# A short arm for a second tile of at most 32 slots in a top-1 mixture of experts, and the last expert's further arms inside its first

## The chip, the cores and the metric

The kernel runs on one core of one Trainium2 chip. The metric is the device time of one execution in microseconds (us), given as the median of timed runs. Each core has five engines with instruction queues of their own: TensorE (PE; its weight loads are listed as PEld), VectorE (DVE), ScalarE (ACT), GpSimd (POOL) and SyncE (SP), which here only issues transfers. A name with a q behind it (PEq, POOLq) is the engine's sequencer, which also carries out branches and semaphore waits.

## The reference

Three stages run one after the other in one launch: attention (2 batches, 8 heads, 576 tokens, head size 64), a dense feed-forward layer (512 to 2048 to 512, ELU), and the mixture of experts, which the change is about. It has 1152 tokens, 8 experts, and a capacity of 288 tokens for each expert:

```python
logits = x @ w_gate                        # [1152, 8]
expert_idx = np.argmax(logits, axis=1)     # one expert for each token
gate_w = probs[np.arange(N), expert_idx]   # softmax of the logits
...                                        # disp[e, s] = the s-th token of expert e, up to capacity
h = np.maximum(np.einsum('ecd,edf->ecf', disp, w1), 0.0)   # 512 -> 1024
y = np.einsum('ecf,efd->ecd', h, w2)                       # 1024 -> 512
out[i] = gate_w[i] * y[expert_idx[i], pos[i]]              # zero for a token over capacity
```

How many tokens an expert gets is known only when the router has run.

## The kernel before, in words

Every product is made from float32 numbers split into a high and a low part, in three passes: high by high, high by low, low by high. A "split" is an ACT copy that makes the high part (`xh`, `gh`, `dh`) and a DVE subtraction that makes the low part (`xl`, `gl`, `dl`, all through the helper at L86).

The dense layer fills the stretch from about 96 to 317 us. There PE and SP follow an order written out by hand, while a scheduler chooses the order of DVE, ACT and POOL; the router's small constants are among what it places, `pair` (L732) with them, a [64, 32] sum of two pieces of the identity.

The experts fill the rest, in an order written out by hand on all engines. POOL writes each token's row (512 numbers, its gate and its index) to its slot in DRAM, `disp`. An expert's 288 slots are cut into tiles of 128, 128 and 32. For each expert `e`:

- SP loads the next expert's first tile of rows (`load_rows(e + 1, 0)`), and half of the weights of the expert after that (`load_x`). Raw weights wait in buffers `ra` and `rb` until they are split.
- `If(count[e] > 0)` (L1333) holds `compute(e, 0)`. PE multiplies 128 slots with the first weights in two halves of 512 columns (L1176, 12 matmuls each), turns the result (L1187), multiplies with the second weights (L1197, 24 matmuls), and between these the engines do side work: the split of the eight weight tiles of expert `e + 1`, `turn_slots(e, 1)` (PE turns the second tile of rows, L1146, ACT makes `dh`, DVE `dl`, POOL copies gate and index into `gt`, L1151 and L1152) and `turn_slots(e + 1, 0)`. The Else arm does the weight splits for an expert without tokens.
- Then SP loads `rows(e + 1, 1)`, into a buffer that POOL's copies of `gt` must have read, and the other half of the weights.
- `If(count[e] > 128)` (L1346) holds `compute(e, 1)`, the same on the second tile with no weights to split beside it. Inside it `If(count[e] > 256)` holds `compute_few(e, 2)` for the third tile: its 32 slots lie twice in one 64-wide operand, `ds`, high parts beside low parts, so that one pass takes the place of two (16, 8 and 16 matmuls: L1244, L1256 with `pair`, L1270).
- POOL sends each tile's result (L1294, an indirect DMA with one index for each slot; empty slots point out of bounds and write nothing).

Each If is a compare on PE, ACT, DVE and POOL apart. Where it is not taken, the engine jumps to a block that raises the semaphores that the skipped block would have raised; on POOL this includes an instruction `INC_SWDGE_SEM` for the skipped send.

## Time and profile before

| | us |
|---|---|
| median of 3 timed runs | 481.84 |
| lowest and highest | 480.65, 484.97 |
| the profiled execution's own time | 480.35 |
| its span, first to last instruction | 478.4 |
| PE busy | 459.9 (96%) |
| DVE busy | 352.1 (74%) |
| ACT busy | 300.1 (63%) |
| POOL busy | 97.9 (20%) |

The profile is of one execution. Its span leaves out some 2 us around the program, so a change of the span is read as the same change of the time. Spans on POOL are rough. Lines are those of the kernel before; the changed kernel's lines stand up to 35 further down.

### The profile page before, as it was taken

Reading aid. Unit: us, or ns where it says so; the run is one execution under the profiler, and the core shown is the slowest. Engines: PE = TensorE matmul, PEld = TensorE weight load, DVE = VectorE, ACT = ScalarE, POOL = GpSimd, SP = SyncE. Lnnn points to the kernel's source line nnn. Section 1 sums busy time; section 2 is a strip of 40 time slices with the busy share of each in tenths; the row PEclk is TensorE's granted clock in tenths of the full one; section 3 lists DMA queues with packets and bytes.
Section 4 is the critical chain, followed back from the end, with each engine's and each line's share of the span. In section 5 each row is a group of like instructions: output and inputs, shape, how many; then the busy total and the mean of one; then the engine's idle time right before and its main releaser. Section 6 shows DMA issues by size and latency. Waiting matters only on the chain. (4 is left out here: it accounts for less than half of the span.)

```text
span 478.4 us, 8177 instructions
## 1 busy us (share of the span) xinstructions
PE 459.9 (96%) x2708; PEld 384.1 (80%) x2708; DVE 352.1 (74%) x765; ACT 300.1 (63%) x660; POOL 97.9 (20%) x178
## 2 busy tenths in 40 slices
PE   7899999999999999999999999999999999999994
PEld 6777777789999999999998888878777877777773
DVE  7999999999989996974473465459388995561661
ACT  5999997967776665653553446447388883541640
POOL 3655666410000000000000020522120331210110
PEclk9999999999999999999999999999999999999999
DMA  7875786036898831330121032448979999260100
GB/s 210 225 205 153 215 249 189 6 135 185 254 299 273 285 135 44 135 130 1 35 99 46 1 110 76 173 130 310 403 241 360 354 357 333 93 228 22 29 27 26
DMA packets 34900, 81.10 MB, mean 170 GB/s; under 512 B 4642, under 2 KB 4642, under 8 KB 34848
## 3 DMA queue, kind: packets, MB, share of 16 engines
q1 hardware_dynamic: 33072, 75.44, 48.8%
q0 software_dynamic: 1632, 4.72, 2.6%
q8 instruction: 27, 0.44, 0.4%
q10 hardware_dynamic: 144, 0.29, 0.2%
q14 instruction: 25, 0.20, 0.2%
HBM read 64.49 MB, written 12.41 MB: 161 GB/s over the span
## 5 line engine op out<-in xcount | busy, mean ns | idle before, releaser
L259 PE MATMUL acc<-wbh,gh 128*128 128x512 f32 x144 | 57.2, 397 | 0.0
L259 PE MATMUL acc<-wbh,gl 128*128 128x512 f32 x144 | 56.8, 394 | 0.0
L259 PE MATMUL acc<-wbl,gh 128*128 128x512 f32 x144 | 56.7, 393 | 0.0
L884 POOL DMA_INDIRECT disp<-y_all,slot x9 | 9.1, 1016 | 198.6 <-DVE e L244 175.9
L242 ACT ACTIVATE e<-h 128x384 f32<-128x384 f32 x48 | 23.2, 484 | 40.1 <-PE h L232 37.7
L185 DVE SCALAR_TENSOR_TENSOR cv_t<-r,cv_t 128x512 int32<-128x512 int32 x64 | 45.4, 710 | 0.5
L452 ACT ACTIVATE prob<-s,stat 64x64 f32<-64x64 f32 (+3 forms) x80 | 41.3, 529 | 6.3 <-PE pT L494 3.0
L232 PE MATMUL h<-xh,wah 128*128 128x384 f32 x192 | 42.7, 342 | 0.6 <-DVE e L244 0.6
L86 DVE TENSOR_TENSOR xl<-ra,xh 128x1024 fp32r<-128x1024 f32 (+1 forms) x36 | 39.2, 1100 | 5.1 <-ACT xh L1096 3.9
L244 DVE SCALAR_TENSOR_TENSOR e<-e,h 128x384 f32<-128x384 f32 x48 | 26.3, 548 | 22.2 <-ACT e L243 21.9
L1096 ACT ACTIVATE xh<-ra 128x1024 fp32r<-128x1024 f32 (+1 forms) x36 | 34.2, 961 | 12.1 <-PEq L1346 8.5
L232 PE MATMUL h<-xh,wal 128*128 128x384 f32 x192 | 41.2, 337 | 0.0
L232 PE MATMUL h<-xl,wah 128*128 128x384 f32 x192 | 41.1, 336 | 0.0
L477 POOL TENSOR_SCALAR prob<-prob,stat 64x64 f32<-64x64 f32 (+2 forms) x64 | 32.6, 521 | 36.5 <-DVE stat L463 14.8
L232 PEld LDWEIGHTS h<-xh,wah 128*128 128x128 f32 x192 | 34.5, 188 | 5.7 <-issue 1.1
L86 DVE TENSOR_TENSOR xl<-rb,xh 128x1024 fp32r<-128x1024 f32 (+1 forms) x36 | 38.8, 1098 | 0.0
L1294 POOL DMA_INDIRECT out<-o,gt x12 | 17.6, 1465 | 100.8 <-DVE o L1229 48.9
L248 ACT ACTIVATE gh<-e 128x384 fp32r<-128x384 f32 x48 | 25.1, 524 | 20.0 <-DVE e L244 18.7
L1197 PE MATMUL acc<-xh,gh 128*128 128x512 f32 x88 | 36.3, 412 | 0.0
L444 DVE TENSOR_REDUCE stat<-s 128x1 f32<-128x320 f32 (+2 forms) x80 | 34.8, 476 | 0.8 <-PE s L426 0.5
L1197 PE MATMUL acc<-xl,gh 128*128 128x512 f32 x88 | 34.7, 395 | 0.0
L1197 PE MATMUL acc<-xh,gl 128*128 128x512 f32 x88 | 34.7, 395 | 0.0
(191 smaller groups left out, 1102.6 us busy)
## 6 DMA issues: line engine op xcount, KB each, us to landing
ra<-in_moe_w SPq DMA_DIRECT2D x32, 512.0 KB, 5.3
rb<-in_moe_w SPq DMA_DIRECT2D x32, 512.0 KB, 5.9
r<-in_moe_w_in SPq DMA_DIRECT2D x16, 512.0 KB, 5.1
r<-in_moe_w_out SPq DMA_DIRECT2D x16, 512.0 KB, 4.4
disp<-z SPq DMA_DIRECT2D x18, 257.0 KB, 6.7
kr<-in_k SPq DMA_DIRECT2D x15, 288.0 KB, 4.0
rows<-disp SPq DMA_DIRECT2D x14, 257.0 KB, 3.4
v<-in_v SPq DMA_DIRECT2D x8, 320.0 KB, 4.5
```

The source lines that it names most:

```text
L86: eng.tensor_tensor(out=lo, in0=x, in1=hi.bitcast(FP32), op=ALU.subtract)
L185: nc.vector.scalar_tensor_tensor(out=st["t"], in0=x(), scalar=scalar, in1=st["t"], op0=op, op1=ALU.bitwise_or)
L232: nc.tensor.matmul(out=h[:, f, :], lhsT=w[:, kk, (f0 + f) * 128:(f0 + f + 1) * 128], rhs=x[:, kk, t0:t0 + n], start=(i == 0), stop=(i == l ...
L242: nc.scalar.activation(out=e, in_=hf, func=ACTF.Relu, scale=-1.0)
L244: nc.vector.scalar_tensor_tensor(out=e, in0=e, scalar=-1.0, in1=hf, op0=ALU.add, op1=ALU.max)
L248: nc.scalar.activation(out=gh, in_=ef, func=ACTF.Copy)
L259: nc.tensor.matmul(out=acc[t], lhsT=x[:, f, t * 128:(t + 1) * 128], rhs=w[:, f0 + f, :], start=(first and f == 0 and i == 0), stop=(last a ...
L444: nc.vector.tensor_reduce(out=stat[n][0][0:nq, t:t + 1], in_=x, axis=AX.X if part else AX.XY, op=ALU.max, negate=True)
L452: nc.scalar.activation(out=out if part else out.rearrange("p (b c) -> p b c", b=NB), in_=x, func=ACTF.Exp, bias=stat[n][0][0:nq, t:t + 1], ...
L477: eng.tensor_scalar(out=p, in0=p, scalar1=sc, scalar2=0.0, op0=ALU.mult, op1=ALU.add)
L1096: lambda: nc.scalar.activation(out=hi, in_=r, func=ACTF.Copy),
L1197: nc.tensor.matmul(out=acc[0:n], lhsT=x[:, f % 4, 0:n], rhs=y[:, f % 2, :], start=(f == 0 and i == 0), stop=(f == NF - 1 and i == 2),)
```

## The change

`FEW = 32` is new. A second tile of 128 slots gets a second operand `ds` (pool `few1`, [128, 4, 64]). `set_aside(1)` fills it with two POOL copies (called CAST in the rows of the order), the first 32 slots of the high and of the low part; it is called once at the start of the experts and then in each `turn_slots(e, 1)`, ahead of the two copies of `gt`. `further(e)` takes the place of the two nested Ifs: a second tile with over 32 tokens in it still gets `compute(e, 1)` and the third tile inside that; one with 1 to 32 gets `compute_few(e, 1)` in an Else. A second `pair` is made for it. For the last expert, `further` is called inside its first If.

```diff
+    FEW = 32
...
         for j, (_, n) in enumerate(FIRST):
-            if n > 64:
+            few = min(n, FEW)
+            if n > FEW:
                 state["dT"].append([pool_of["cnt"].tile([128, KD, n], F32R, name=f"d{x}{j}") for x in "hl"])
+            else:
+                both = state["dS"][j] = pool_of["cnt"].tile([128, KD, 2 * n], F32R, name=f"ds{j}")
+                state["dT"].append([both[:, :, 0:n], both[:, :, n:2 * n]])
+            if j == 0:
                 continue
...
+            n = few
             pair = state["pair"][j] = pool_of["cnt"].tile([2 * n, n], FP32, name=f"pair{j}")
...
+    def set_aside(j):
+
+        if j in state["dS"] and FIRST[j][1] > FEW:
+            for x, src in enumerate(state["dT"][j]):
+                nc.gpsimd.tensor_copy(
+                    out=state["dS"][j][:, :, x * FEW:(x + 1) * FEW], in_=src[:, :, 0:FEW].bitcast(FP32)
+                )
...
+        for j, (s0, n) in enumerate(stiles):
+            if j and n > FEW:
+                dS[j] = p3.enter_context(tc.tile_pool(name=f"few{j}", bufs=1, side="right")).tile(
+                    [128, KD, 2 * FEW], F32R, name=f"ds{j}"
+                )
+                set_aside(j)
...
             split_lo(nc.vector, lo, ps[:, :, 0:n], hi)
+            set_aside(j)
             nc.gpsimd.tensor_copy(out=gt[0:n, j, 0:1], in_=r[0:n, DM:DM + 1])
...
+        def further(e, j=1):
+
+            if j == CT:
+                return
+            s0, n = stiles[j]
+            with tc.If(count[e] > s0):
+                if n <= FEW:
+                    compute_few(e, j)
+                    return further(e, j + 1)
+                with tc.If(count[e] > s0 + FEW) as many:
+                    compute(e, j)
+                    further(e, j + 1)
+                with many.Else():
+                    compute_few(e, j)
...
             with tc.If(count[e] > 0) as some:
                 compute(e, 0, (his, los[:-LATE]), turn_next)
+                if not new:
+                    further(e)
...
-            with ExitStack() as arms:
-                for j in range(1, CT):
-                    arms.enter_context(tc.If(count[e] > 128 * j))
-                    (compute_few if j in dS else compute)(e, j)
+            if new:
+                further(e)
```

The program's order shows what this makes of three places. The first is PE between the fifth expert's first arm and the sixth expert's. Before, the second tile has one way to be computed; the rows are the start of that arm (`dh_1706` and `dl_1707` are the second tile's operands):

```order
L1346 COMPARE_AND_BRANCH
L1176 MATMUL hx<-xh,dh_1706 128x512 x4
L1176 MATMUL hx<-xl,dh_1706 128x512 x4
L1176 MATMUL hx<-xh,dl_1707 128x512 x4
L1146 MATMUL dT<-ident,rows 128x32 x4
L1176 MATMUL hx<-xh,dh_1706 128x512 x4
L1176 MATMUL hx<-xl,dh_1706 128x512 x2
```

Now that arm is followed by a second one in the program, on PE again, the start and end of which are (`ds_4045` is the new operand, `pair_1708` its pair):

```order
L1341 UNCONDITIONAL_BRANCH x2
L1264 MATMUL hx<-xh,ds_4045 64x512 x4
L1264 MATMUL hx<-xl,ds_4045 64x512 x4
L1264 MATMUL hx<-xh,ds_4045 64x512 x4
L1276 MATMUL hT<-pair_1708,hr 128x32 x4
L1264 MATMUL hx<-xl,ds_4045 64x512 x4
L1290 MATMUL acc<-xh,gh 64x512
...
L1345 UNCONDITIONAL_BRANCH
L1341 UNCONDITIONAL_BRANCH
L1368 COMPARE_AND_BRANCH
L1196 MATMUL hx<-xh,dh_1704 128x512 x4
```

The short arm stands in every expert's piece of the program, behind the long one, so an engine that skips both has more instructions to jump over. The turn of the third tile's rows (`dT<-ident,rows 128x32`) stands in the long arm alone.

The second place is POOL at the start of an expert's first arm, before:

```order
L1333 COMPARE_AND_BRANCH
L1151 COPY gt<-rows 128x1
L1152 COPY gt<-rows 128x1
L1151 COPY gt<-rows 128x1
L1152 COPY gt<-rows 128x1
L1294 DMA out<-o,gt 1152x512
```

and now:

```order
L1368 COMPARE_AND_BRANCH
L772 CAST ds_4045<-dh_1706 128x4x32
L772 CAST ds_4045<-dl_1707 128x4x32
L1171 COPY gt<-rows 128x1
L1172 COPY gt<-rows 128x1
L1171 COPY gt<-rows 128x1
L1172 COPY gt<-rows 128x1
L1314 DMA out<-o,gt 1152x512
```

The two casts stand ahead of the first copies of `gt`, so these wait for the second tile's `dl` too.

The third is DVE early in the dense layer, where the scheduler places the router's constants, before:

```order
L732 TENSOR_TENSOR pair_1709<-ident 64x32
L697 TENSOR_TENSOR add<-add,ident 128x8
L86 TENSOR_TENSOR wal<-cv_t,wah 128x512
L244 SCALAR_TENSOR_TENSOR e<-e,h 128x384
L697 TENSOR_TENSOR add<-add,ident 128x8
```

and now:

```order
L737 TENSOR_TENSOR pair_1708<-ident 64x32
L698 TENSOR_TENSOR add<-add,ident 128x8
L737 TENSOR_TENSOR pair_1711<-ident 64x32
L86 TENSOR_TENSOR wal<-cv_t,wah 128x512
L244 SCALAR_TENSOR_TENSOR e<-e,h 128x384
L698 TENSOR_TENSOR add<-add,ident 128x8
```

The second `pair` stands ahead of the `e` that PE's next product is made from. Behind this place the scheduler has exchanged neighbours on DVE and ACT for a part of the dense layer; the order of PE and SP there is the same as before.

## Rows read from the trace of the kernel before

**Rows 1.** The page's head: span, then busy time, share and instructions of each engine.

```profile
span 478.4 us, 8177 instructions
PE 459.9 (96%) x2708; PEld 384.1 (80%) x2708; DVE 352.1 (74%) x765; ACT 300.1 (63%) x660; POOL 97.9 (20%) x178
```

**Rows 2.** POOL's DMA queue (packets, MB, share) from 411.3 and from 448.6 us.

```profile
q0 software_dynamic: 80, 0.00, 0.4%
q0 software_dynamic: 32, 0.07, 2.5%
```

**Rows 3.** Windows: length; busy PE, PEld, DVE, ACT, POOL (count); clock; DMA share; GB/s.

```profile
383.87:396.90 13.03, 13.03 (x64) 10.68 (x65) 12.29 (x13) 10.90 (x14) 4.09 (x5) 1.00 1.01 364
396.90:410.26 13.36, 12.80 (x61) 9.85 (x60) 5.15 (x7) 2.99 (x6) 2.14 (x3) 1.00 0.82 293
409.00:411.00 2.00, 1.44 (x7) 0.88 (x6) 0.75 (x1) 1.17 (x2) 0.00 (x0) 1.00 0.03 9
435.92:445.64 9.72, 9.72 (x50) 6.13 (x48) 1.33 (x3) 1.71 (x4) 0.98 (x1) 1.00 0.07 27
```

**Rows 4.** Timeline of PE: start, us, engine, line, operation, shapes; idle before and releaser.

```profile
356.33 0.49 PE L1176 MATMUL hx<-xh,dh 128*128 128x512 f32 x1 [0.31 <-PEq L1346]
...
410.26 0.49 PE L1176 MATMUL hx<-xh,dh 128*128 128x512 f32 x1 [0.56 <-PEq L1346]
...
445.64 0.39 PE L1176 MATMUL hx<-xh,dh 128*128 128x512 f32 x1
```

**Rows 5.** The second Ifs' line: sequencer operation, count, ns min/median/max, first and last start.

```profile
L1346 PEldq COMPARE_BRANCH  x16: 65/179/424, 327.3 to 472.2; - x16
L1346 POOLq INC_SWDGE_SEM  x7: 389/443/580, 343.8 to 475.2; - x7
```

**Rows 6.** Timeline of DVE at the constants, and of PE behind it.

```profile
102.30 0.33 DVE L732 TENSOR_TENSOR pair<-ident 64x32 f32<-64x32 f32 x1
...
103.23 0.53 DVE L244 SCALAR_TENSOR_TENSOR e<-e,h 128x384 f32<-128x384 f32 x1
...
103.82 0.45 PE L232 MATMUL h<-xh,wah 128*128 128x384 f32 x1 [0.57 <-DVE e L244]
```

**Rows 7.** A window of the dense layer, its columns as in rows 3.

```profile
100.00:180.00 80.00, 79.43 (x403) 71.97 (x402) 75.91 (x160) 55.90 (x111) 1.62 (x3) 1.00 0.73 228
```

**Rows 8.** A group of POOL by form: busy us, mean ns, idle before and releasers.

```profile
L477 POOL TENSOR_SCALAR prob<-prob,stat 128x192 f32<-128x192 f32 x8 | 3.4, 426 | 20.9 <-DVE stat L463 14.8 <-PE xT L528 3.6 <-PE s L426 2.5
```

**Rows 9.** Timeline of POOL and of DVE in the fifth expert's first arm.

```profile
386.39 0.32 POOL L1151 COPY gt<-rows 128x1 f32<-128x1 f32 x1
...
390.92 0.81 POOL L1151 COPY gt<-rows 128x1 f32<-128x1 f32 x1 [4.10 <-DVE gl L86]
391.67 1.20 POOL L1152 COPY gt<-rows 128x1 int32<-128x1 int32 x1
...
389.26 0.68 DVE L86 TENSOR_TENSOR dl<-dT,dh 128x512 fp32r<-128x512 f32 x1
...
390.47 1.22 DVE L86 TENSOR_TENSOR xl<-ra,xh 128x1024 fp32r<-128x1024 f32 x1
391.61 1.22 DVE L86 TENSOR_TENSOR xl<-rb,xh 128x1024 fp32r<-128x1024 f32 x1
```

**Rows 10.** Timeline of SP's queue in the fifth expert, and of ACT in the sixth.

```profile
387.95 0.52 SPq L1139 DMA_DIRECT2D rows<-disp  x1
391.75 1.43 SPq L96 DMA_DIRECT2D ra<-in_moe_w  x2
...
417.62 1.06 ACT L1096 ACTIVATE xh<-ra 128x1024 fp32r<-128x1024 f32 x1
```

**Rows 11.** POOL's last send (timeline), and the program's last line (columns as rows 5).

```profile
473.00 0.98 POOL L1294 DMA_INDIRECT out<-o,gt  x1 [10.99 <-issue]
...
L1398 POOLq DRAIN  x3: 46/102/1792, 475.8 to 478.1; - x3
```

**Rows 12.** The page's DMA queues: packets, MB, share of 16 engines' span.

```profile
q8 instruction: 27, 0.44, 0.4%
```

## The prediction, made before the changed kernel had run

> **What bounds the kernel now.** I read the page's head first: PE is busy for 459.9 of 478.4 us, 96% [rows 1], so time is won only where PE has fewer instructions or waits less. For the experts I then cut the span into windows, one for each arm, at the first matmul of each as PE's timeline gives it. The reader is to see that PE's column equals the window's length in most of them: the fifth expert's first arm takes 13.03 us, all of them PE's, its second arm 13.36 with 12.80 of PE, and the one short arm that runs today (sixth expert, third tile) 9.72, all PE's [rows 3]. The clock column is 1.00 in each, so PE's clock doesn't differ between the arms that are compared. What is left are the gaps at the Ifs: 0.31 us of idle PE ahead of the third expert's first arm, where a second arm had been jumped over, 0.56 ahead of the sixth expert's, where a third tile's had been, and none where an arm ran to its end [rows 4].

> **Whom the change reaches.** The short arm is for a second tile with 1 to 32 tokens. POOL's queue tells how many tokens a send wrote, at 2 KB each: a full tile is 0.26 MB. The send of the fifth expert's second tile moved 0.00 MB as the page rounds, so at most two tokens; the third tile that ran moved 0.07 MB, 32 tokens [rows 2]. Every other second tile that ran sent a full tile's bytes. So one arm of the whole program changes, the one from 396.90 to 410.26 us.

> **The parts and their cost.**

> 1. That arm: 13.36 us out, 9.72 in [rows 3]: **-3.64**. Both figures hold the way into the arm and the way out to the next expert. The old arm's includes the 0.56 gap of the third tile's If. The short arm's ends as today's does: the next expert's first matmul has no idle time before it [rows 4], since the short arm now runs to its end and its jump back is PE's sequencer's business ahead of PE. The way in differs: a jump past the long arm where today's short arm is fallen into. Bounds: nothing (the compare is done while PE has matmuls queued; its median is 179 ns [rows 5]) and the 0.56 of the costliest gap [rows 4]. I take nothing, as the sequencer is ahead of PE when no semaphore of PE's own is waited for.

> 2. Is the next arm ready 3.64 us sooner? The sixth expert's weights are split already. Its first arm splits the seventh's; their loads have ended by 409 (DMA share 0.03 from there [rows 3]), and the fifth of its eight splits, the first to need the later half of them, ran at 417.62 [rows 10], now 413.98. So 5 us are left, and this costs nothing; without that cover it would cost what the load is late.

> 3. The second `pair`: 0.33 us of DVE, just ahead of the `e` (103.23) for which PE waits 0.57 at 103.82 [rows 6]. DVE is late there already, so it goes on in full: **+0.3**. From there to 180 us DVE is busy 75.91 of 80 us, PE 79.43 [rows 7], so neither regains much. Behind it DVE's and ACT's neighbours are exchanged by the scheduler. Best case: the 0.57 wait goes altogether; worst: it doubles. So -0.6 to +0.9.

> 4. Two casts in each of six first arms, on POOL, of 128 columns by 128 partitions. No such cast is in the trace; the nearest row is a POOL pass over 192 columns, 426 ns [rows 8], and beside DVE's `xl` a POOL copy of a single column took 0.81 and 1.20 us, not the 0.32 it took alone [rows 9]. So a cast takes 0.3 to 1.2 us, and both end 0.6 to 2.4 us behind `dl`, which ends at 389.94 [rows 9]. Behind them on POOL stand the copies of `gt`. For these SP waits: its `rows` load at 387.95 goes out 2 to 3.5 us later, and the loads of weights behind it in SP's queue, at 391.75 [rows 10], by some 0.6 at most. Those rows are turned in the next expert's first arm and those weights split there, and an arm is 13 us long [rows 3]: hidden, 0. Without that cover it would be the 0.6 in each of five experts, 3 us. The short arm itself needs the casts at 396.9, 4 us behind their end: 0.

> 5. The casts against DVE. DVE has 12.29 of 13.03 us of work in that arm [rows 3], so what the casts take from it would count. The trace: two `xl` took 1.22 each with a POOL copy beside them, and the copies were what stretched [rows 9]: 0. [...]

> 6. More compares (one more in an expert with a second tile), ahead of PE at a median of 179 ns [rows 5]: 0. In the last expert the second If's false side goes: POOL passes one compare and one `INC_SWDGE_SEM` of 443 ns [rows 5] less between its last send (473.00) and the drain at 475.8, whose 1.79 us wait for the program's end [rows 11]. Bounds 0 (the send's own landing ends last) to -0.4; I take **-0.2**.

> Sum: -3.64 + 0.3 - 0.2 = **-3.5 us**. The profiled execution took 480.35, so 476.8. It stands 1.49 under the median of the timed runs and 0.30 under their lowest; the median of all four executions is 481.25, and I set the sum against that: **477.7**. The sum's own ends are -3.64 - 0.6 - 0.4 = -4.6 and -3.64 + 0.6 + 0.9 + 0.2 = -2.0 (0.2 for a compare that shows): 476.6 to 479.3.

> **Rivals.**

> - *Jumps that PE feels.* Getting into the short arm and past it cost a gap of 0.56 and one more of 0.31 to 0.56 at the first and sixth experts' ends, which have a new jump past the short arm: +0.6 to +1.7, say +1.4: 479.1. For it: gaps stand where code is jumped over [rows 4]. Against: there the engine waits in the empty block, and the new jumps have none. 0.09.
> - *Casts that hold DVE.* Two casts of 0.43 [rows 8] block `xl` in the three first arms that follow each other without a second arm between (third to fifth expert), where DVE has little to spare [rows 3]: 3 x 0.86 = +2.6, and -0.9 is left: 480.3. For it: the copies' stretching shows that the two engines do meet [rows 9]. Against: only POOL lost. 0.08.
> - *The longer program, slower than before.* In every expert the short arm adds instructions to what is jumped over. If each such jump waits for a fetch of instructions that today's shorter jumps escape, PE stands for it. The rows price a packet of the instruction queue: 0.4% of 16 engines for 478.4 us over 27 packets [rows 12] is an estimate of 0.004 x 16 x 478.4 / 27 = 1.13 us. Six experts with a jump ahead of the last one: +6.8, so +3.3 net: 484.5. It decides from 3.5 / 6 = 0.6 us a jump on. Against: jumps past whole arms are made today, and leave 0.31 to 0.56 with a semaphore's wait in them [rows 4]. [...] 0.06.
> - *It doesn't do what it says* (the fifth expert has over 32 tokens in its second tile after all): only +0.3 and -0.2 remain, 481.3. Against: 0.00 MB [rows 2]. 0.02.

> The forecast has the remaining 0.75. **Range:** the forecast's own ends, widened by half of the 1.49 between the executions of before, take in the first rival and reach the second: 475.6 to 480.3.

> **Chances.** 1% is 4.8 us, about what a measurement can tell from no change. The forecast's 3.5 is 0.7%; its best end is 4.6, so it takes a favourable end and a favourable scatter to pass: 0.18. Slower by over 1% needs the third rival at its dearest, or something not named here: 0.03. Within 1%: 0.79.

> **What would show it.** In the changed profile: the fifth expert's second arm on PE should read near 9.7 us, with `ds` as its operand and no idle time at either end (step 1, first rival); the next expert's splits wait for no load (2); the wait for `e` near 104 us reads 0.8 to 0.9 and the experts begin 0.3 us later (3); the first arms of the third to fifth expert keep their lengths, and `xl` its 1.22 (4, 5, second rival); gaps ahead of the second, third and fourth expert keep their size (third rival); and the stretch behind the last matmul is 6.6 to 7.0 us (6). I am wrong if the part before the experts moves by more than 1 us, or if that arm isn't shorter by 3 us.

## The result, and the profile after

The changed kernel takes 476.94 us in the median of 16 runs, the kernel before 482.94 in 16 runs beside them; the ratio is 0.9889, with a 95% interval of 0.9868 to 0.9910. That is 4.3 to 6.4 us less, where the forecast's sum was 3.5 us less. The time lies in the range (475.6 to 480.3), 0.8 us under the forecast.

The profiled execution of the changed kernel is not one of its quickest: 479.48 us. Its head, and the rows that answer to [rows 1] and [rows 12]:

```profile
span 477.8 us, 8163 instructions
PE 461.4 (97%) x2696; PEld 384.5 (80%) x2696; DVE 351.4 (74%) x766; ACT 300.4 (63%) x660; POOL 102.0 (21%) x190
...
q8 instruction: 30, 0.49, 0.4%
```

By the span alone the change would have won 0.6 us. So the first thing to do is to cut the span at the experts' first matmul; ahead of it the change adds only the second `pair` and exchanges neighbours on DVE and ACT. Before it stands at 317.52, so 160.9 us are left to the end; now it stands at 321.13, and 156.7 are left. The experts' stretch is 4.2 us shorter, and the stretch ahead of it was 3.6 us longer in this one execution. The windows say why:

```profile
16.00:20.00 4.00, 3.24 (x18) 2.61 (x19) 2.75 (x12) 3.04 (x9) 2.71 (x6) 0.61 0.78 198
317.50:320.50 3.00, 3.00 (x14) 3.00 (x14) 0.43 (x3) 0.00 (x0) 2.39 (x3) 0.50 0.48 181
```

The last three columns are the granted clock, the DMA share and GB/s. The clock stood at 0.61 in the first window, after a wait of 1.74 us for a load of attention, and at 0.50 in the second, after the router's matmuls with waits of 0.51 and 0.33 us among them; these matmuls then started every 0.24 us, not every 0.13. In the profile of before the clock stayed at 1.00 at both places. Its wait for that load was 0.67 us, but at the router it had the same two waits of 0.51 and 0.33, so these alone don't explain the fall. An execution's own luck with the clock is as large as the whole change, which is why the stretches are compared below and not the spans.

The arms that answer to [rows 3] (window length, busy PE, PEld, DVE, ACT, POOL, clock, DMA share, GB/s): the fifth expert's first, its second, which is now the short one, and the sixth expert's third tile.

```profile
387.99:401.03 13.04, 13.04 (x64) 10.63 (x65) 11.30 (x12) 10.91 (x14) 2.56 (x7) 1.00 1.01 363
401.03:410.75 9.72, 9.72 (x50) 6.13 (x49) 3.60 (x5) 1.72 (x4) 1.72 (x1) 1.00 0.35 126
436.29:445.95 9.66, 9.66 (x49) 6.12 (x48) 1.33 (x3) 1.72 (x4) 0.98 (x1) 1.00 0.08 29
```

PE's timeline at their starts, beside [rows 4]; a bracket is the idle time before, with what ended it:

```profile
387.99 1.19 PE L1196 MATMUL hx<-xh,dh 128*128 128x512 f32 x4 [1.42 <-PEq L1341]
...
401.03 1.10 PE L1264 MATMUL hx<-xh,ds 128*64 128x512 f32 x4
...
410.75 1.09 PE L1196 MATMUL hx<-xh,dh 128*128 128x512 f32 x4
```

The short arm takes 9.72 us, to the hundredth what the third tile's took before, and is free of idle time at both ends. But ahead of the arm before it stands a gap of 1.42 us that was 0.31. PE's sequencer explains it (columns: operation, count, ns min/median/max, start); first the changed kernel there, then the kernel before:

```profile
L1341 PEldq COMPARE_BRANCH  x1: 3977/3977/3977, 383.7 to 383.7; - x1
```

```profile
L1346 PEldq COMPARE_BRANCH  x1: 334/334/334, 380.6 to 380.6; - x1
```

The compare of the fourth expert's second If, not taken, lasted 3.98 us, not 0.33. It began 2.7 us before PE ran out of queued matmuls (the last started at 386.17), so only the rest shows. In the same window, 383.7 to 387.7 us, the instruction queue moved one packet (packets, MB, share):

```profile
q8 instruction: 1, 0.02, 1.7%
```

That is what the third rival describes, a jump that waits for instructions; the experiments are to show whether it is so.

### The profile page after: what moved, and what is told of

Read it like the earlier page. It is cut to its first block, busy times and chain, and to the rows that moved or that the text cites. A ratio compares the mean times of both kernels' runs of the same rounds, so it can differ in the third digit from the quotient of the medians.

```text
span 477.8 us, 8163 instructions
## 1 busy us (share of the span) xinstructions
PE 461.4 (97%) x2696; PEld 384.5 (80%) x2696; DVE 351.4 (74%) x766; ACT 300.4 (63%) x660; POOL 102.0 (21%) x190
## 5 line engine op out<-in xcount | busy, mean ns | idle before, releaser
L232 PEld LDWEIGHTS h<-xl,wah 128*128 128x128 f32 x192 | 34.0, 188 | 0.0
L232 PEld LDWEIGHTS h<-xh,wal 128*128 128x128 f32 x192 | 34.0, 188 | 0.0
L1109 ACT ACTIVATE xh<-rb 128x1024 fp32r<-128x1024 f32 (+1 forms) x36 | 33.5, 955 | 0.0
```

The lines of the kernel that those rows point to most:

```text
L232: nc.tensor.matmul(out=h[:, f, :], lhsT=w[:, kk, (f0 + f) * 128:(f0 + f + 1) * 128], rhs=x[:, kk, t0:t0 + n], start=(i == 0), stop=(i == l ...
L1109: lambda: nc.scalar.activation(out=hi, in_=r, func=ACTF.Copy),
```

## The experiments

Every kernel ran beside the kernel before on one chip. Two measures are used: the ratio with its interval, and, because the clock scatters so, the time at a granted clock of 0.995. The latter comes from one slope, 3.4 us for each 0.01 of a run's mean granted clock, fitted to the runs of all kernels together, with a level for each kernel. It is an estimate. By it the kernel before stands at 481.1 to 482.0 in the four sets of runs that were taken of it beside the others, each to 0.4 to 0.6, the changed kernel at 477.2 +- 0.5 in its first runs. "Experts' stretch" is from their first matmul to the end of the span, in the one profiled execution; "tail" from the start of the last matmul plus 0.24 us (the matmuls ahead of it start every 0.23).

**The changed kernel again** (no edit).

> The changed kernel itself, for a second profile. First theory (the gain is the short arm, -3.64, and the program's end, -0.9 as its first profile shows it; the one gap of 1.42 us ahead of the fifth expert's first arm, where TensorE's sequencer stood for 3.98 us in a compare, is a fetch of instructions that loses a race with the weights' transfers and need not come each time): the experts' stretch from the first matmul to the end of the span is 155.5 to 156.8 us, against 160.65 before, the gap is between 0.31 and 1.5. Rival (a gain in the dense layer from the exchanged order on DVE and ACT): the stretch from the wait for e near 104 us to the experts' first matmul is 1 us or more shorter than the 213.9 of before.

Ratio 0.9902 (0.9867 to 0.9938); 477.8 at that clock. The stretch is 155.95 us. The gap is there again, at 0.78, with a compare of 3.30 us:

```profile
L1341 PEldq COMPARE_BRANCH  x1: 3297/3297/3297, 382.9 to 382.9; - x1
```

So the wait belongs to the kernel, not to one execution. The stretch from the wait for `e` to the experts was 214.3, no shorter than before's 213.7: no gain in the dense layer.

**The long arm always.**

```diff
-                with tc.If(count[e] > s0 + FEW) as many:
+                with tc.If(count[e] > s0) as many:
```

> The second If's inner test always holds, so the long arm runs for the fifth expert too; the program is as long as the changed one, instruction for instruction. First theory: 3.6 us slower than the changed kernel, so still 0.9 to 1.8 faster than before (ratio 0.996 to 0.998), from the end alone. Rival (the order of the dense layer gives 2 us): ratio about 0.994. Second rival (the longer program costs time at jumps): ratio 1.000 or above, with gaps over 1 us at the jumps.

Ratio 0.9961 (0.9936 to 0.9985), 481.2 at that clock. The arm is back at 13.47 us:

```profile
397.52:410.99 13.47, 12.81 (x61) 9.86 (x60) 5.26 (x7) 3.10 (x6) 2.15 (x3) 1.00 0.80 284
```

The ratio lies where the first theory had it, though its interval holds the rival's 0.994 too; the time is 3.4 to 4.0 us above the changed kernel's at equal clock. The stretch is 160.16, 3.5 to 4.2 more than with the short arm, and the long compare (3.64 us, gap 1.06) is there too. All else together, the end and what the longer program loses, is worth 0.6 to 0.7 us by the stretch.

**The last expert's further arms outside its first If again**, as before.

```diff
                 compute(e, 0, (his, los[:-LATE]), turn_next)
-                if not new:
-                    further(e)
...
-            if new:
-                further(e)
+            further(e)
```

> The last expert's further arms stand outside its first If again, all else as changed. First theory: the end of the program, from the last matmul to the end of the span, is 0.9 us longer, 6.9 to 7.0 as before, and the time 0.9 above the changed kernel's (ratio about 0.991). By the prediction's term (-0.2): 0.2 above, ratio 0.9895.

Ratio 0.9928 (0.9897 to 0.9959), 478.6 at that clock, so about 1 us slower, nearer the first expectation's 0.9 than the other's 0.2, but the intervals of the two kernels overlap. The tail tells them apart: it is 6.88 us against 6.26 and 6.23 in the changed kernel's two profiles, and 7.17 and 7.18 before: the nesting gives 0.65, and 0.3 comes from the rest of the change. The changed kernel's end, beside [rows 11]:

```profile
473.32 0.98 POOL L1314 DMA_INDIRECT out<-o,gt  x1 [10.97 <-DVEq L1368]
...
L1433 POOLq DRAIN  x3: 46/102/1935, 475.0 to 477.5; - x3
```

From the last send to the drain it is 1.7 us now and was 2.8; the drain grew by only 0.14.

**One pair for both tiles**, so that nothing is added in the dense layer.

```diff
             n = few
+            if state["pair"] and n == FEW:
+                state["pair"][j] = state["pair"][1]
+                continue
```

> The second pair is the third tile's own, which holds the same numbers; no instruction is added ahead of the experts, and the order of DVE and ACT in the dense layer is that of before. First theory: the extra pair costs 0 to 0.3, so the ratio is 0.9885 +- 0.002, as the changed kernel's. Rival (the exchanged order gives 2 us): 2 us slower than the changed kernel, ratio about 0.993.

Ratio 0.9875 (0.9841 to 0.9908), 477.4 at that clock: as the changed kernel, so the exchanged order is not the missing gain. An interval of 1.6 us to either side is too coarse for the 0.3 that the pair was to cost; PE's own wait must tell. PE's wait for `e` was 0.75 us without the extra operation, 0.52 and 0.84 with it, 0.57 and 0.73 in the two profiles of before: no price to be seen, within a scatter as large as the price. (In its one profile the fifth expert's short arm lasted 10.29 us, with PE stopped in the middle of a group of turns; the next experiment meets that kind of stop in the kernel before.)

**The kernel before again** (no edit).

> The kernel before, for a second profile of it and the granted clock of each of its runs. First theory (what the changed kernel won beyond the sum is the program's end, plus scatter of TensorE's granted clock, which was lower in the runs of before, 0.990 in the mean against 0.993): the stretch from the experts' first matmul to the end of the span is 160.6 to 161.2 us again, with a tail of 6.9 to 7.2 and no gap over 0.65 at a jump; and a time within 1 us of 481.9 at a clock of 0.995. Rival (before has a stall in another stage that the change took away): a stretch ahead of the experts that is longer than in the changed kernel's profiles at the same clock.

Ratio 0.9981 (0.9951 to 1.0012), 481.6 at that clock. The stretch is 160.76, the tail 7.18. The experts begin at 320.34, against 320.35 in the changed kernel's second profile: no stall ahead of them that the change took away. Both profiles of before share a thing that the prediction had passed over: their third expert's first arm lasts 14.02 and 13.99 us, the changed kernel's 13.50. PE stops in the middle of a group of four turns, for nothing that another engine does:

```profile
362.00 0.27 PE L1146 MATMUL dT<-ident,rows 128*128 128x128 f32 x1
362.52 0.55 PE L1146 MATMUL dT<-ident,rows 128*128 128x128 f32 x3 [0.25 <-issue]
```

The bracket's "issue" says that PE waited there for no semaphore that the profile shows. The 0.5 us that the arm lost there are gone in the changed kernel, which has its loss at a jump instead.

**The short arm in the fifth expert's code alone.** The other experts' code is that of before.

```diff
+                if e != 4:
+                    compute(e, j)
+                    return further(e, j + 1)
                 with tc.If(count[e] > s0 + FEW) as many:
```

> The changed kernel with the short arm for a second tile in the fifth expert's code alone, the one that takes it; the other experts' code is that of before (the last one's still nested). First theory (TensorE waits for instructions at a jump that has become too long): the gap ahead of the fifth expert's first arm falls from 0.65 to 1.42 back to 0.31, no sequencer's compare there takes over 0.5 us, and the experts' stretch is 155.2 to 155.6 us. Rival (the gap is a semaphore's, from POOL's two casts or SP's later loads, which all stay): it stays above 0.6.

Ratio 0.9892 (0.9851 to 0.9933), 477.3 at that clock. Every jump's gap is 0.31 to 0.55, the compare is 0.33 us, no arm has an idle time, and casts and loads are as in the changed kernel: the gap is no semaphore's. This run shortens the jumps and moves the code as well, so it doesn't tell length from place. The stretch was forecast at 155.2 to 155.6 and is 156.06, since the tail is 6.66 and not 6.2: POOL's first `INC_SWDGE_SEM` at the end comes 0.3 us later than in the changed kernel, and the drain lasts 0.1 longer; why, no run tells.

**A program meant to be longer still.**

```diff
                     compute_few(e, j)
+                    with tc.If(count[e] > 2 * CP):
+                        compute_few(e, j)
                     return further(e, j + 1)
```

> The changed kernel with one more short arm in each expert's code, behind the third tile's in the same If, under a test that never holds. First theory (length of the jump): gaps of 0.6 us or more ahead of the fifth expert's first arm and of at least one of the third's and fourth's, each with a compare of over 1 us in TensorE's sequencer; beside them some 0.5 for the extra test that is not taken behind the sixth expert's third tile; together 1 to 4 us slower than the changed kernel. [...]

The experiment missed its aim: a test above the largest count can't hold, so the extra arm was dropped from the program, and a branch or two for each expert is all that is left: the instruction queue moved 30 packets, as in the changed kernel, and 33 in the run below, where the arm stays. It still told something. Ratio 0.9903 (0.9869 to 0.9937), 478.6 at that clock; with all later code a few instructions further down, the compare ahead of the fifth expert fell from 3.30 to 2.68 us, and the gap to 0.31. The time is no lower for it: the extra branch shows as a gap of 0.68 behind the sixth expert's third tile, and the fourth's first arm and the fifth's short arm lose some 0.5 together. With a test that has to be made in the run, the arm stays:

```diff
+                    with tc.If(count[e] < s0):
```

> The changed kernel with one more short arm behind the third tile's in the same If of each expert, under a test that never holds but that can't be dropped ahead of the run (the earlier one, with a test above the capacity, was dropped, and left a branch or two for each expert). Jumps past the second tile's arms are some 40 matmuls and their loads longer. Theory of the jump's length: gaps of 0.6 or more at two or three of the second to fifth expert's starts. Theory of the place: one such idle time as before, anywhere, 0.2 to 1.1 us. Both: some 0.5 to 0.8 at the sixth expert's end for the test that isn't taken.

Ratio 1.0147 (1.0095 to 1.0199): slower than before. Two compares took 6.68 and 4.80 us, with gaps of 4.12 and 2.31 at the third and fourth expert and an idle time of 2.58 inside the fifth's first arm. By their sizes both theories' forecasts were too small. As the longer arm also moves all later code, this run doesn't show that length did it; the next four keep the length and move the code.

**The same work at another place.** The first expert's Else never runs here; more turns in it only push all later code down. P is the number of turns added: 8, 16, 5 and 20, in the order of the expectations.

```diff
                         f()
-                    turn_next()
+                    for _ in range(1 if e else P + 1):
+                        turn_next()
```

> The changed kernel; in the first expert's Else, which never runs, the turn of the next expert's rows stands nine times instead of once. It runs the same instructions, but all code behind stands 32 matmuls and their weight loads further down. First theory (TensorE's sequencer waits for a block of instructions where a block's start falls at a place with little queued ahead of TensorE, so the place decides): the gap ahead of the fifth expert's first arm (0.65 to 1.42 so far) changes by over 0.3 us or goes, and an idle time of 0.2 to 1 turns up elsewhere in the experts, or none; the experts' stretch lies between 155.2 and 157.2. Rival (the length of the jump decides, which is the same as in the changed kernel at each later jump): the gap is 0.65 to 1.42 at the same place.

> As the one before with 17 turns, so 64 matmuls and their weight loads further down. First theory: again another place or size of that idle time, and if it falls under a full queue, gaps of 0.31 alone at the third to fifth expert and a stretch of 155.2 to 155.6, with a time 0.5 to 1 under the changed kernel's at the same clock. Rival: the gap as in the changed kernel.

> The changed kernel with six turns instead of one in the first expert's Else, which never runs: all later code 20 matmuls and their loads (40 instructions) further down. Theory of the place, fitted to the earlier profiles (a jump waits if its target lies past the block of instructions that is next; one instruction or three further down had already taken the fifth expert's compare from 3.3 to 2.7 us): the compare ahead of the fifth expert's first arm takes under 0.5 us and the gap is 0.31 there and at the third and fourth; no idle time inside the arms; experts' stretch 155.3 to 155.8 us; time 0.4 to 1.0 under the changed kernel's at the same clock. If the fit is wrong: a compare over 2.5 us at one of the three jumps, or an idle time inside the arm behind one.

> As the one before with 21 turns: 80 matmuls and their loads (160 instructions) further down. By the same fit: the compare ahead of the fourth expert's first arm takes over 3 us, with a gap of 0.6 to 4 there, and the ones ahead of the third and fifth stay under 0.5; the time 1 to 5 us above the changed kernel's, more where TensorE's clock falls behind the gap. If the fit is wrong: the long compare stands elsewhere or there is none.

| P | ratio (interval) | at 0.995 | experts' stretch | compares ahead of the 3rd, 4th, 5th expert, us | idle inside an arm |
|---|---|---|---|---|---|
| 0 (changed) | 0.9902 (0.9867 to 0.9938) | 477.8 | 155.95 | 0.3, 0.3, 3.3 | none |
| 5 | 0.9885 (0.9839 to 0.9931) | 477.3 | 156.05 | 0.3, 0.3, 0.4 | 0.3 |
| 8 | 0.9972 (0.9942 to 1.0002) | 480.1 | 157.59 | 0.3, 0.3, 0.3 | 1.68 |
| 16 | 1.0102 (1.0067 to 1.0138) | 484.6 | 167.45 | 5.4, 7.0, 0.3 | 0.70 |
| 20 | 1.0129 (1.0086 to 1.0173) | 485.8 | 167.35 | 4.1, 6.2, 5.3 | none |

All five run the same instructions, with jumps of the same length at every later expert. The place of the code alone moves the time from 1.1% under before to 1.3% over it. With P at 16 the sequencer's longest compare, and PE and the clock behind it:

```profile
L1341 PEldq COMPARE_BRANCH  x1: 6959/6959/6959, 370.9 to 370.9; - x1
```

```profile
373.80:378.15 4.35, 0.00 (x0) 0.01 (x1) 3.02 (x3) 0.19 (x1) 1.72 (x1) 0.91 0.76 288
378.15:384.00 5.85, 5.85 (x15) 4.58 (x16) 2.36 (x2) 2.09 (x3) 0.00 (x0) 0.50 0.74 232
```

PE stands for 4.35 us, and for 5.85 us behind that it runs at 0.50. So the price of this gap is paid twice. That the place decides held, with the rival (the length decides, so the gap stays where it was) refuted by P at 5, 8 and 16. The sizes missed: with P at 8 the idle time is 1.68 us and the stretch 157.59, where at most 1 and 157.2 were forecast; with P at 16 the stretch is 167.45, where 155.2 to 155.6 was the forecast for the good case and none was made for so bad a one. The fit that was to say which jump waits failed too. With P at 5 the three compares were short as forecast, but the stretch is above its 155.3 to 155.8 and the time is the changed kernel's within the interval, for the fourth expert's first arm keeps 0.3 us of idle time, and the long compare has only moved, to the jump into the fifth expert's short arm:

```profile
L1345 PEldq COMPARE_BRANCH  x1: 2549/2549/2549, 394.8 to 394.8; - x1
```

The matmuls queued there hide all of it but 0.2 us. With P at 20 the fit named one jump and 1 to 5 us; three jumps waited, and the time is 8.0 us above the changed kernel's 477.8.

## Why the prediction was right, point by point

*The arm* (step 1, -3.64): 13.36 became 9.72, 9.75 in the second profile, so -3.6; the way in by a jump cost nothing, as taken, and the first rival didn't happen. (At another place of the code, P at 5, the way in cost 0.2.) That one arm changes is shown by the run with the long arm, which gives 3.5 to 4.2 us of the stretch back.

*The next arm's readiness* (2): the sixth expert's first arm is 12.93 and 12.87 us long, not longer than 13.05: nothing waited.

*The extra pair* (3, +0.3): not to be seen; the run without it shows no difference, but couldn't show one of 0.3. In the changed kernel a `pair` takes 0.17 us, and the next operation starts 0.1 behind it.

*Casts* (4, 5): 0.29 us each, mostly, on POOL:

```profile
392.28 0.29 POOL L772 CAST ds<-dh 128x128 fp32r<-128x128 f32 x1 [2.86 <-ACT dh L1168]
393.06 0.29 POOL L772 CAST ds<-dl 128x128 fp32r<-128x128 f32 x1 [0.49 <-DVE dl L86]
393.30 0.18 POOL L1171 COPY gt<-rows 128x1 f32<-128x1 f32 x1
```

The first arms kept their lengths (13.04 and 13.02 in the fifth expert against 13.03), and DVE's `xl` its 1.22 us. Hidden, as said; the second rival didn't happen. Two casts in each profile took 1.35 us (in the third and fourth experts' first arms), above the 1.2 that I had as the most. Each cast that met an `xl` in the two profiles began inside it and ended 0.1 to 0.2 us behind its end, so POOL still loses where the two meet. None began ahead of an `xl` and lasted into it; whether `xl` would be held then, no run shows.

*The end* (6, -0.2, bounds 0 to -0.4): mis-sized. The tail fell by 0.9 us, of which the nesting gives 0.65. I had set the end by the send's landing as much as by POOL's own work, and had priced an `INC_SWDGE_SEM` at its median of 443 ns, where those of the end take 0.56 to 0.59 us. The drain started 1.1 us earlier in relation to the send, and lasted 0.14 longer: POOL's sequencer was the path, nearly alone.

*The jumps* (first and third rival): the wait that the third rival describes came at one jump of six, and costs 0.3 to 1.1 us in the five profiles that have the changed kernel's code at this place, the same edits or nearly (gaps of 0.65 to 1.42 in place of 0.31). Its price was wrong: I took 1.13 us, the time of a packet, at each jump. The packet does take about that (0.88 to 1.20 us), but the wait also holds what passes before the packet starts and the 1.3 to 1.6 us after it ends. What was measured is a compare of 3.2 to 4.0 us, of which the matmuls already queued hide some 2.7 to 2.9. And I had not seen that the kernel before pays for the same thing, 0.5 us inside the third expert's first arm, which the change takes away. That it is a wait for instructions is read from the runs: one packet of the instruction queue stood in each long compare, compares in PE's sequencer took either at most 0.5 us or 2.5 to 7.0, and which it was hung on the code's place. How the place decides it, no run here shows.

*The sum.* By the experts' stretches: -3.6 for the arm, -0.9 for the end, -0.5 for the third expert's arm, +0.3 to +1.1 at the jump, which is -3.9 to -4.7; measured, 160.8 to 160.9 became 155.95 and 156.67, so -4.1 to -4.9. At equal clock the times differ by 3.3 to 4.8 us, which agrees. The rest of the 4.3 to 6.4 is, by the estimate from the slope, the clock: it was 0.990 in the mean over 70 runs of before, 0.994 and 0.992 in the changed kernel's 16 and 9, which makes 0.7 to 1.3 us. Why before should have the lower clock stays open: the execution of before that the prediction read had none of the slow stretches, and the second profile has two, at the start and ahead of the experts, as the changed kernel's first has; the changed kernel's second has one, at the start.

*What was luck.* The time fell 0.8 us from the forecast because two misses met. The forecast stood on 481.25 us for the kernel before, and beside the changed kernel its median was 482.94, so 1.7 more; and the medians differ by 6.0 us, not 3.5. The 3.5 lies outside the interval's 4.3 to 6.4. The change passed 1% by the middle value (1.1%, interval 0.9 to 1.3), for which the prediction had given a chance of 0.18. The stated range, 475.6 to 480.3, is a little wider than its own rule makes it (the sum's ends widened by 0.75 are 475.9 and 480.0); the time lies in either. Last, one of the signs of being wrong came up, a part before the experts that moves by more than 1 us: it was 3.6 longer. That sign was set inside the scatter, as the kernel before itself begins its experts at 317.52 in one profile and 320.34 in the other.

## What to carry to other kernels

Cut the span where the edit cannot reach and compare the stretches behind it: an execution's luck ahead of the cut was 3.6 us here, nearly as large as the change. Price code in a branch that is not taken by the sequencer's compares: a jump that usually took 0.3 us here could take 2.5 to 7, and edits that only shifted later code, in a part that never runs, switched that on and off. So when a change to control flow is timed, look at the longest compare of each engine, and try one or two paddings before judging the edit.

## What the runs showed of the hardware

Two of the long compares were nearly alike under very different traffic. The compare of 3.98 us stood beside a DMA share of 1.04, that of 3.45 us, after the last arm, beside 0.21; the packet in it took 1.10 us in the one and 1.09 in the other:

```profile
383.70:387.70 4.00, 2.87 (x13) 2.00 (x12) 3.61 (x5) 2.50 (x3) 0.00 (x1) 1.00 1.04 407
472.10:475.60 3.50, 0.00 (x0) 0.00 (x0) 0.44 (x1) 0.00 (x0) 0.98 (x1) 0.81 0.21 80
```

```profile
L1368 PEldq COMPARE_BRANCH  x1: 3452/3452/3452, 472.1 to 472.1; - x1
```

The second costs nothing, as POOL's drain ends later. Two more things. The longest compares (6.7 and 7.0 us) are about twice the common one, and yet hold one packet of q8 each, no longer than the others; it starts 4.3 and 4.6 us into the compare, not 0.8 to 1.5. What holds it back, no run shows. And PE's clock fell to 0.50 for several us at each of the seven stops of 2.3 to 4.4 us in the experts (with P at 16 it was 0.66 in the mean of the 4.96 us behind the stop of 2.83, and 0.50 for the 5.85 behind that of 4.36), but not at those of 1.42 (the changed kernel), 1.68 (P at 8) and 1.74 (P at 20); in attention it fell behind a wait of 1.74 (0.61 in the window from 16 to 20 us above), so the length of one stop doesn't decide it alone.
